# Weight pieces converted in blocks of two, and attention values split straight from PSUM, in an attention + mixture kernel

## The chip, the cores and the metric

The kernel runs on one core of a Trainium2 chip. The metric is the device time of one execution in microseconds (us). Before the change it is 828.13 us, the median of three runs (827.27 to 829.08). The core has a matrix engine (TensorE, PE in the profile; its weight loads are the row PEld), three engines for elementwise work (VectorE or DVE, ScalarE or ACT, GpSimd or POOL) and a queue that issues transfers between memory and the core (SyncE, SP). All of them run side by side, each in its own fixed order, and wait for each other through semaphores. Matmul results land in a memory of their own, PSUM; all other tiles lie in SBUF.

## The reference

There are 8 batches of 8 heads. Each head has 512 local and 32 global tokens of 64 numbers. A global token attends to all keys of its head; a local token attends to the 32 global keys and to the local keys at most 32 positions away. The result, laid out as 8 x 544 rows of 512, goes through three first-layer matrices whose maximum is taken, and one second-layer matrix:

```python
s_g = scale * np.matmul(q_g, k_all.transpose(0, 1, 3, 2))
out_g = np.matmul(sm(s_g), v_all)
mask = np.abs(pos[:, None] - pos[None, :]) <= window
s_l = np.concatenate([s_lg, np.where(mask, s_ll, -1000000000.0)], axis=-1)
out_l = np.matmul(sm(s_l), np.concatenate([v_g, v_l], axis=2))
...
h = np.maximum(np.maximum(x @ w1, x @ w2), x @ w3)   # 512 -> 768
return (h @ w_out).astype(np.float32)                # 768 -> 512
```

The four weight matrices arrive as 64-bit floating-point numbers (they are drawn as float32 and then multiplied with a float64 scale), and everything else as 32-bit.

## The kernel before, in words

**Split numbers.** Most products are made from operands of the type F32R (`fp32r` in the rows). The kernel splits an operand into a high part (a copy of that type) and a low part (the operand minus its high part), and a product is the sum of three matmuls: high x high, high x low, low x high. `copy` (line 105) makes the high part on ACT or DVE; `sub` (line 98) makes the low part on DVE or POOL, and on DVE alone if an operand lies in PSUM. Which engine is chosen is decided while the program is built: `least` (line 86) adds the cost of each choice to running loads of ACT ("a"), DVE ("d"), POOL ("p") and of a resource "x", counted by operations of DVE and POOL on SBUF, and takes the least. From the 26th tile on the first choice is always taken.

**Attention.** The work is cut into 128 tiles: a tile is one pair of heads and 128 of the 512 local queries. `SEQ` (line 209) is their order; in the first batch (16 tiles, `EARLY`) it is two tiles of each of the four head pairs, then the other two of each. The loop at line 567 does in iteration i, for tile SEQ[i]: transpose the probabilities of tile i+1 (`trans`, four PE transposes into one PSUM bank T, one copy to SBUF); score tile i+3 (`next_scores`, `scores`: matmuls into one of two PSUM banks S, then on DVE a masked row-minimum with L342, exponentials on ACT with L344, sums and reciprocals on DVE with L347 and L348, and a normalisation by `times`); multiply the probabilities of tile i with the values (`pv`, line 391: matmuls into O, a PSUM tile with one buffer, copied out into `xr`); load later queries, keys and values; run the weight steps; and split the attention output. From the second batch on the probabilities also make a way through a DMA (L351) before they are transposed.

**Matmuls of the mixture.** `moe_local(b)` is a generator that yields after each matmul; `fill(n)` takes n of them, 21 an iteration in the first 32 iterations (6, 5, 3 and 7). For batch 0 it starts in iteration 8 and does layer 1 for 256 columns, then for the other 256: 18 first-layer pieces, 12 matmuls each, over six tiles h0 to h5; then layer 2 with six second-layer pieces. It reads the attention output from `xs[0][p]`, one tile for each head pair, with a high and a low plane of 512 columns. In the first batch `split_x` makes it in every odd iteration, 256 columns of `xr` at a time: one `copy` and one `sub`.

**Weights.** Each of the 24 pieces is 128 x 512 float64 numbers (512 KB) and is turned into a split pair (`convert`, line 169): ACT takes the absolute value of the upper halves (L175); DVE clamps and shifts (L176, L177); one step later DVE merges the sign and the lower bits in (L180, L181); another step later a `copy` and a `sub` write the high and the low part over the raw piece. Scratch for the first 18 pieces is a pair of tiles that lie in h4 and h5, which layer 1 doesn't need yet, and for the last six the output buffers. `weight_step` (line 192) takes every piece in work one step on, begins the next and loads one more. `WS` (line 526) says how many weight steps an iteration makes: one in most, two in iterations 6, 10 and 14. Four pieces are loaded ahead of the loop, and a load of piece n waits for the ACT conversion of piece n-5.

**Order.** The program is written in the order above; while it is built a scheduler orders the instructions of each engine by that order and by when it estimates that their inputs are ready. So matmuls of the mixture can come ahead of attention work that isn't ready, and the lists on the engines follow the text only roughly.

## Time and profile before

| | |
|---|---|
| median of three runs | 828.13 us (827.27 to 829.08) |
| the profiled execution: its time, its span | 831.31 us, 829.5 us |
| busy time of PE | 803.7 us (97% of the span) |
| busy time of DVE, ACT, POOL | 616.8, 508.5, 459.2 us |
| share of the 16 DMA engines' time that the transfers of q1 took | 37.5% |
| DVE busy in the first 100 us, in fifths | 13.20, 19.65, 18.20, 19.54, 17.30 of 20 us each |
| PE busy in the same fifths | 14.13, 15.70, 17.60, 18.77, 17.87 |
| granted clock of PE in the same fifths | 1.00, 1.00, 0.83, 1.00, 0.91 |

Rows of a profile name a line of the kernel, an engine, the operation and its tiles, output first: `S<-kh,qn` is a score matmul that reads keys and queries. A bracket at the end of a timeline row is the idle time of the engine just before it and who ended it. `x18: 661/671/703` is a count, and least, median and longest duration in ns. DVE overlaps the end of one operation with the start of the next, so that a row's duration is somewhat longer than the distance to the next row's start (0.41 us against 0.33 where one at 23.70 us is followed by the next at 24.03). All times count from the start of the span.

### The profile page before, as it was taken

To read this page: it belongs to the slowest core of one execution; us is meant where nothing else is said; L and a number is where in the kernel's file an instruction comes from. 1 tells how busy PE (TensorE), PEld (TensorE's weight loads), DVE (VectorE), ACT (ScalarE), POOL (GpSimd) and SP (SyncE) were. 2 spreads that over 40 slices of the span, in tenths; PEclk is the share of its full clock that TensorE was granted. 3 is DMA by queue.
4 is the path that set the end of the run, shared out by engine and by line. 5 is a ranking of instruction groups with operands and counts; after the bars stand their busy time and mean duration, and the time that the engine had idled before them with its cause. 6 is when DMAs were issued, how large, how long until landed. Compare 5 with 4: busy or idle time off the path is not lost.

```text
span 829.5 us, 16594 instructions
## 1 busy us (share of the span) xinstructions
PE 803.7 (97%) x4772; PEld 685.8 (83%) x4772; DVE 616.8 (74%) x2192; ACT 508.5 (61%) x1415; POOL 459.2 (55%) x624
## 2 busy tenths in 40 slices
PE   7788999999999999999999999999999999999996
PEld 5577888888888888888888888888888888888895
DVE  6999897878888888888897888888887887421121
ACT  5987786657666766667676667666676766311110
POOL 4223345756677676756676676866786665311110
PEclk9989999999999999999999999999999999999999
DMA  9856554433334433343335333443325332100101
GB/s 309 304 185 212 167 152 148 139 127 115 109 115 136 121 92 112 99 151 102 104 109 166 116 98 92 133 138 110 93 88 166 115 93 74 61 1 1 38 14 26
DMA packets 97467, 98.16 MB, mean 118 GB/s; under 512 B 19296, under 2 KB 85856, under 8 KB 97376
## 3 DMA queue, kind: packets, MB, share of 16 engines
q1 hardware_dynamic: 97232, 96.87, 37.5%
q8 instruction: 38, 0.62, 0.3%
q14 instruction: 53, 0.43, 0.2%
q10 hardware_dynamic: 144, 0.23, 0.1%
HBM read 60.39 MB, written 8.91 MB: 84 GB/s over the span
## 4 chain that ended last, share of the span: by engine, by line
PE 86%; DMA 5%; issue 3%; DVE 2%; SPq 1%; ACT 1%; POOL 1%; POOLq 0%; DVEq 0%; ACTq 0%
PE pm L441 48%; PE pm L463 17%; PE O L409 7%; PE S L339 5%; PE T L362 2%; DMA prob<-s 2%; DMA raw<-w_in 2%; PE T L363 2%; PE S L289 2%; PE S L335 1%; DMA vraw<-v_in 1%; PE S L381 1%; PE O L401 1%; POOL w L103 1%; DMA qn<-q_in 1%
## 5 line engine op out<-in xcount | busy, mean ns | idle before, releaser
L441 PE MATMUL pm<-xs,w 128*128 128x512 f32 (+1 forms) x2160 | 488.9, 367 | 1.3 <-ACT m L115 0.9
L441 PEld LDWEIGHTS pm<-xs,w 128*128 128x128 f32 x2160 | 355.9, 191 | 52.7 <-issue 4.2
L463 PE MATMUL pm<-w,h 128*128 128x512 f32 x612 | 156.4, 396 | 0.0
L103 POOL TENSOR_TENSOR h<-m,h 128x512 fp32r<-128x512 f32 (+1 forms) x59 | 70.6, 1197 | 109.8 <-ACT h L115 109.2
L463 PEld LDWEIGHTS pm<-w,h 128*128 128x128 f32 x612 | 109.4, 188 | 19.1 <-issue 0.2
L450 DVE TENSOR_TENSOR m<-pm,m 128x512 f32<-128x512 f32 (+1 forms) x120 | 72.8, 607 | 63.1 <-PE pm L441 62.3
L344 ACT ACTIVATE s<-s,nm 128x192 f32<-128x192 f32 (+1 forms) x224 | 103.3, 462 | 22.3 <-DVE nm L342 17.6
L103 POOL TENSOR_TENSOR qs<-qraw,qs 128x256 fp32r<-128x256 f32 x100 | 76.5, 765 | 69.1 <-issue 33.2
L125 POOL TENSOR_SCALAR s<-s,z 128x224 f32<-128x224 f32 (+1 forms) x194 | 84.9, 446 | 36.5 <-ACT lox L115 18.9
L342 DVE CUSTOM_DVE_ANT_0 s<-S,mask 128x192 f32<-128x192 f32 (+1 forms) x224 | 74.8, 370 | 16.3 <-PE S L339 7.7
L103 POOL TENSOR_TENSOR vs<-vraw,vs 128x256 fp32r<-128x256 f32 x102 | 75.0, 736 | 13.3 <-ACT vs L115 6.5
L103 DVE TENSOR_TENSOR pt<-T,pt 128x512 fp32r<-128x512 f32 x102 | 70.4, 690 | 15.2 <-ACT pt L115 13.8
L409 PEld LDWEIGHTS O<-pt,vs 128*128 128x128 f32 x408 | 65.9, 188 | 10.4 <-issue 2.4
L409 PE MATMUL O<-pt,vs 128*128 128x320 f32 (+1 forms) x408 | 73.1, 300 | 1.4 <-DVE pt L103 1.4
L115 ACT CAST pt<-T 128x512 fp32r<-128x512 f32 x102 | 60.3, 592 | 16.6 <-PE T L363 14.0
L339 PEld LDWEIGHTS S<-kst,qs 128*128 128x128 f32 x400 | 59.6, 190 | 8.7
L417 DVE TENSOR_TENSOR xr<-O,lox 64x160 f32<-64x160 f32 x204 | 64.3, 315 | 2.9
L103 POOL TENSOR_TENSOR kst<-kraw,kst 64x576 fp32r<-64x576 f32 x44 | 63.9, 1453 | 4.3 <-PE S L335 1.0
L115 ACT CAST h<-m 128x512 fp32r<-128x512 f32 (+1 forms) x59 | 33.2, 562 | 52.8 <-DVE m L450 52.5
L115 ACT CAST qs<-qraw 128x256 fp32r<-128x256 f32 x93 | 38.0, 409 | 44.0 <-PE S L339 31.1
L339 PE MATMUL S<-kst,qs 128*128 128x192 f32 (+1 forms) x400 | 59.5, 270 | 0.0
L347 DVE TENSOR_SCALAR z<-z 128x1 f32<-128x1 f32 x256 | 37.2, 147 | 27.3 <-ACT s L344 18.7
(123 smaller groups left out, 1183.0 us busy)
## 6 DMA issues: line engine op xcount, KB each, us to landing
vraw<-v_in SPq DMA_DIRECT2D x122, 128.0 KB, 2.3
qraw<-q_in SPq DMA_DIRECT2D x100, 128.0 KB, 2.1
prob<-s SPq DMA_DIRECT2D x56, 224.0 KB, 2.5
raw<-w_in SPq DMA_DIRECT2D x24, 512.0 KB, 4.9
prob<-s SPq DMA_DIRECT2D x56, 192.0 KB, 2.3
out_dram<-o SPq DMA_DIRECT2D x32, 256.0 KB, 2.6
kraw<-k_in SPq DMA_DIRECT2D x25, 320.0 KB, 3.1
qn<-q_in SPq DMA_DIRECT2D x29, 128.0 KB, 3.7
```

Source lines behind the costliest of these rows:

```text
L103: (dve if least(c) == "d" else pool).tensor_tensor(out=out, in0=a, in1=b, op=ALU.subtract)
L115: act.copy(out=out, in_=a)
L125: pool.tensor_scalar(out=out, in0=a, scalar1=col, scalar2=1.0, op0=ALU.mult, op1=ALU.mult)
L339: pe.matmul(ph[j][:, 0:n], lhsT=qs[sl][:, a, 128 * j:128 * j + 128], rhs=kst[p][:, j, c0:c0 + n], start=(a == 0), stop=(a == 1))
L342: dve.tensor_tensor_reduce(out=s[:, j, 0:n], in0=ph[j][:, 0:n], in1=mask[:, (1, 0, 1, 0)[t], 32 * (t == 0):32 * (t == 0) + n], scale=-0.12 ...
L344: act.activation(out=s[:, j, 0:n], in_=s[:, j, 0:n], func=AF.Exp, bias=nm[:, j:j + 1], scale=-1.0, accum_out=z[:, j:j + 1])
L347: dve.tensor_scalar(out=z[:, j:j + 1], in0=z[:, j:j + 1], scalar1=1e-9, scalar2=None, op0=ALU.add)
L409: pe.matmul(o[:, j, 0:320].rearrange("p (a q) -> p a q", a=2)[:, :, 0:n], lhsT=vs[sl][:, 2 * j + c].rearrange("p a d -> p (a d)"), rhs=pt[ ...
L417: dve.tensor_tensor(out=xr[p][64 * j:64 * j + 64, t], in0=o[0:64, j, 0:160], in1=lo[:, j], op=ALU.add)
L441: pe.matmul(ps[:, 0:n], lhsT=weight(3 * f + i, w)[:, 128 * k:128 * k + 128], rhs=xs[k][:, a, c0:c0 + n], start=(q == 0), stop=(q == 11))
L450: dve.tensor_tensor(out=m[:, 0:n], in0=ps[:, 0:n], in1=m[:, 0:n], op=ALU.max)
L463: pe.matmul(banks[t], lhsT=hh[f][:, a, 128 * t:128 * t + 128], rhs=weight(18 + f, w), start=((f, a, w) == (0, 0, 0)), stop=((f, w) == (5, 1)))
```

## The change

**Weights.** The 18 first-layer pieces are loaded, converted and kept in nine blocks of two; the six second-layer pieces stay single. A block is one transfer of 1 MB, one ACT operation, four DVE operations, one `copy` and one `sub`, each over 1024 columns in place of two over 512. The scratch of block k is a fresh tile in h3, h4 or h5, by the list `PLACE`. A load of block k waits for the ACT conversion of block k-3, two blocks are loaded ahead of the loop in place of four pieces, and the next load goes out only in an iteration that begins a block. `weight_step` runs once in each iteration, and `WS` now lists the iterations that begin a block. What `convert` tells the planner it spends is changed to fit.

**First batch's values.** `pv` for the first 16 tiles no longer copies O into `xr`. It takes the tile's 128 columns of `xs[0][p]`: a `copy` out of PSUM writes the high plane, and a `sub` that reads O in PSUM and the high plane writes the low plane. The eight calls of `split_x` in the odd iterations go.

```diff
@@ -148,59 +148,66 @@
     raw, wt = {}, {}
 
     def weight(n, a):
-        return wt[n][:, 512 * a:512 * a + 512]
+        if n < 18:
+            return wt[n // 2][:, n % 2, 512 * a:512 * a + 512]
+        return wt[n - 9][:, 0, 512 * a:512 * a + 512]
 
     xg = const.tile([128, NP, B, SG], F32, name="xg")
     turned = psT.tile([128, 512], F32, name="T")
     dve.memset(turned, 0.0)
 
-    spare = [moe.tile([128, 2, 512], I32, name="spare", tag=f"h{f}") for f in (4, 5)]
+
+    PLACE = [3, 4, 5, 3, 4, 3, 5, 4, 5]
     loaded, marks = [0], {}
 
     def load_weight():
-        n = loaded[0]
-        if n < 24:
+        k = loaded[0]
+        if k < 15:
             loaded[0] += 1
-            raw[n] = const.tile([128, 512], mybir.dt.int64, name=f"raw{n}", tag=f"w{n}")
-            d = nc.sync.dma_start(out=raw[n], in_=win[n])
-            if n >= 6:
-                tc.add_manual_dep(d.ins, marks[n - 5], SYNC, reason="pace")
-
-    def convert(n):
-        r = raw[n].bitcast(I32).rearrange("p (n t) -> p n t", t=2)
-        if n < 18:
-            c = spare[n // 2 % 2 if n < 15 else 1][:, n % 2]
-        else:
-            c = moe.tile([128, 512], I32, name="wct", tag="o", bufs=2)
-        marks[n] = act.activation(out=f32(c), in_=f32(r)[:, :, 1], func=AF.Abs).ins.name
+            m = 2 if k < 9 else 1
+            raw[k] = const.tile([128, m, 512], mybir.dt.int64, name=f"raw{k}", tag=f"w{k}")
+            if m == 2:
+                d = nc.sync.dma_start(out=raw[k], in_=win[2 * k:2 * k + 2].rearrange("t p x -> p t x"))
+            else:
+                d = nc.sync.dma_start(out=raw[k][:, 0], in_=win[k + 9])
+            if k >= 3:
+                tc.add_manual_dep(d.ins, marks[k - 3], SYNC, reason="pace")
+
+    def convert(k):
+        r = raw[k].bitcast(I32).rearrange("p j (n t) -> p j n t", t=2)
+        if k < 9:
+            c = moe.tile([128, 2, 512], I32, name="wct", tag=f"h{PLACE[k]}")
+        else:
+            c = moe.tile([128, 1, 512], I32, name="wct", tag="o", bufs=2)
+        m = 2 if k < 9 else 1
+        marks[k] = act.activation(out=f32(c), in_=f32(r)[:, :, :, 1], func=AF.Abs).ins.name
         dve.tensor_scalar(out=f32(c), in0=f32(c), scalar1=2.0 ** -15, scalar2=HIMAX, op0=ALU.max, op1=ALU.min)
         dve.tensor_scalar(out=c, in0=c, scalar1=0x07FFFFFF, scalar2=3, op0=ALU.bitwise_and, op1=ALU.logical_shift_left)
-        spend("a", 520)
+        spend("a", 427 * m + 98)
         yield
-        dve.scalar_tensor_tensor(out=c, in0=r[:, :, 1], scalar=-0x40000000, in1=c, op0=ALU.bitwise_and, op1=ALU.bitwise_or)
-        dve.scalar_tensor_tensor(out=c, in0=r[:, :, 0], scalar=29, in1=c, op0=ALU.logical_shift_right, op1=ALU.bitwise_or)
-        spend("dx", 1900)
+        dve.scalar_tensor_tensor(out=c, in0=r[:, :, :, 1], scalar=-0x40000000, in1=c, op0=ALU.bitwise_and, op1=ALU.bitwise_or)
+        dve.scalar_tensor_tensor(out=c, in0=r[:, :, :, 0], scalar=29, in1=c, op0=ALU.logical_shift_right, op1=ALU.bitwise_or)
+        spend("dx", 1600 * m + 300)
         yield
-        wt[n] = const.tile([128, 1024], F32R, name=f"w{n}", tag=f"w{n}")
-        copy(weight(n, 0), f32(c))
-        sub(weight(n, 1), f32(c), f32(weight(n, 0)))
+        t = wt[k] = const.tile([128, m, 1024], F32R, name=f"w{k}", tag=f"w{k}")
+        copy(t[:, :, 0:512], f32(c))
+        sub(t[:, :, 512:1024], f32(c), f32(t)[:, :, 0:512])
         yield
 
-    todo = iter(range(24))
+    todo = iter(range(15))
     live = []
 
-    def weight_step():
+    def weight_step(begin):
         for c in list(live):
             next(c[0])
             c[1] += 1
             if c[1] == 3:
                 live.remove(c)
-        n = next(todo, None)
-        if n is not None:
-            c = convert(n)
+        if begin:
+            c = convert(next(todo))
             next(c)
             live.append([c, 1])
-        load_weight()
+            load_weight()
 
 
     NS = 4 * B * NP
@@ -392,15 +399,21 @@
         p, t = divmod(sl, 4)
         pt = pts.pop(sl)
         o = psO.tile([128, 2, 512], F32, name="O")
-        if t == 0:
+        if t == 0 and sl < EARLY:
+            xs.setdefault(0, []).append(x_tile())
+        elif t == 0:
             xr[p] = xp.tile([128, 4, 160], F32, name="xr")
         if sl < NAT:
 
             for c, j in ((0, 0), (0, 1), (1, 0), (1, 1)):
                 n = 160 if sl >= EARLY and c < GCH[t][2] else 128
                 pe.matmul(o[64 * j:64 * j + 64, 0, 0:n], lhsT=vraw[sl][:, 2 * j + c], rhs=pt[:, j, c, 0:n], start=(c == 0), stop=(c == 1))
-            n = 160 if sl >= EARLY else 128
-            copy(xr[p][:, t, 0:n], o[:, 0, 0:n], True)
+            if sl < EARLY:
+                x = xs[0][p]
+                copy(x[:, 0, 128 * t:128 * t + 128], o[:, 0, 0:128], True)
+                sub(x[:, 1, 128 * t:128 * t + 128], o[:, 0, 0:128], f32(x)[:, 0, 128 * t:128 * t + 128], True)
+            else:
+                copy(xr[p][:, t], o[:, 0, 0:160], True)
         else:
 
             for j in range(2):
@@ -523,7 +536,7 @@
 
     mm = [None]
 
-    WS = [1, 1, 1, 1, 1, 1, 2, 1, 1, 1, 2, 1, 1, 1, 2, 1, 1, 1, 1, 1, 1, 1, 1, 1]
+    WS = [0, 2, 4, 6, 7, 9, 10, 12, 14, 15, 16, 17, 18, 19, 20]
 
     def fill(n):
         if mm[0]:
@@ -556,13 +569,11 @@
     load_v(SEQ[1], 1)
     load_weight()
     load_half(2)
-    load_weight()
     next_scores(1)
     load_v(SEQ[2], 2)
     load_weight()
     next_scores(2)
     load_v(SEQ[3], 3)
-    load_weight()
     trans(SEQ[0])
     for i, sl in enumerate(SEQ):
         p, t = divmod(sl, 4)
@@ -608,13 +619,8 @@
             load_v(tile_at(i + 4), i + 4)
         else:
             load_v(tile_at(i + 4))
-        for _ in range(WS[i] if i < len(WS) else 0):
-            weight_step()
+        weight_step(i in WS)
         if i < 16:
-            if i % 2:
-                if i < 8:
-                    xs.setdefault(0, []).append(x_tile())
-                split_x(xr[p][:, 2 * (i // 8):2 * (i // 8) + 2, 0:128], xs[0][p], 256 * (i // 8), 256)
             if i == 7:
                 mm[0] = moe_local(0)
         elif i % 16 >= 12:
```

## The prediction

> **What bounds the kernel now.** The page comes first: TensorE (PE) is busy 97% of the span, so the whole run is worth at most the 25.8 us in which it isn't, and work taken from another engine counts only where PE waits for it.
>
> ```profile
> span 829.5 us, 16594 instructions
> PE 803.7 (97%) x4772; PEld 685.8 (83%) x4772; DVE 616.8 (74%) x2192; ACT 508.5 (61%) x1415; POOL 459.2 (55%) x624
> ```
>
> The view by stretches says where that is. Columns: stretch, its length, busy us of PE, PEld, VectorE (DVE), ScalarE (ACT), GpSimd (POOL), granted clock, DMA share, GB/s.
>
> ```profile
> 0.00:17.00 17.00, 11.13 (x67) 9.21 (x68) 10.25 (x54) 9.26 (x29) 6.01 (x22) 1.00 0.89 300
> 17.00:38.60 21.60, 18.04 (x125) 12.54 (x123) 21.20 (x73) 18.95 (x53) 6.23 (x7) 1.00 0.94 323
> 38.60:43.50 4.90, 1.75 (x13) 1.17 (x14) 4.90 (x15) 3.92 (x11) 1.62 (x1) 0.88 0.36 129
> 43.50:50.60 7.10, 7.10 (x35) 6.55 (x35) 7.10 (x27) 6.21 (x18) 2.25 (x2) 0.61 0.25 76
> 50.60:75.00 24.40, 24.00 (x184) 20.52 (x184) 22.60 (x79) 20.33 (x59) 6.07 (x7) 1.00 0.78 258
> 75.00:100.00 25.00, 22.05 (x160) 18.15 (x159) 21.84 (x74) 17.57 (x54) 8.36 (x8) 0.93 0.57 180
> 165.00:820.00 655.00, 654.48 (x3672) 561.13 (x3671) 473.94 (x1663) 386.25 (x1062) 390.43 (x534) 1.00 0.32 98
> ```
>
> From 165 us on PE has no gap; nothing this change touches lies there. From 17 to 50.6 us DVE is the full engine (33.2 of 33.6 us). After PE's idle stretch at 38.6 the granted clock is 0.61 over 7.1 us, 2.8 us of PE work lost; 75 to 100 loses 1.8 (0.07 of 25).
>
> The timeline of PE shows what it waits for.
>
> ```profile
> 35.57 0.65 PE L401 MATMUL O<-pt,vn 128*64 128x128 f32 x6
> 38.62 0.66 PE L401 MATMUL O<-pt,vn 128*64 128x128 f32 x8 [0.84 <-ACT xr L115]
> 40.63 1.02 PE L335 MATMUL S<-kh,qn 128*128 128x224 f32 x4 [1.36 <-DVE nm L342]
> 43.43 0.47 PE L362 MATMUL T<-one,early 128*128 128x128 f32 x1 [1.77 <-ACT early L123]
> 60.83 0.44 PE L401 MATMUL O<-pt,vn 128*64 128x128 f32 x4 [0.38 <-ACT xr L115]
> 80.08 0.62 PE L441 MATMUL pm<-xs,w 128*128 128x256 f32 x3 [0.91 <-ACT m L115]
> 82.37 0.28 PE L362 MATMUL T<-identr,prob 128*128 128x128 f32 x1 [1.67 <-DMA prob<-s]
> 95.05 0.26 PE L362 MATMUL T<-identr,prob 128*128 128x128 f32 x1 [0.35 <-DMA prob<-s]
> ```
>
> And the timeline of DVE says why: the first row-minimum (L342) of tiles 9, 10, 11, 13, 14, 15 and 17, counted in the order of work.
>
> ```profile
> 33.67 0.34 DVE L342 CUSTOM_DVE_ANT_0 early<-S,mask 128x192 f32<-128x192 f32 x1
> 39.87 0.38 DVE L342 CUSTOM_DVE_ANT_0 early<-S,mask 128x224 f32<-128x224 f32 x1
> 43.96 0.34 DVE L342 CUSTOM_DVE_ANT_0 early<-S,mask 128x192 f32<-128x192 f32 x1
> 52.12 0.35 DVE L342 CUSTOM_DVE_ANT_0 early<-S,mask 128x192 f32<-128x192 f32 x1
> 59.63 0.38 DVE L342 CUSTOM_DVE_ANT_0 early<-S,mask 128x224 f32<-128x224 f32 x1
> 64.43 0.34 DVE L342 CUSTOM_DVE_ANT_0 early<-S,mask 128x192 f32<-128x192 f32 x1
> 73.13 0.39 DVE L342 CUSTOM_DVE_ANT_0 s<-S,mask 128x224 f32<-128x224 f32 x1
> ```
>
> Tile 11 comes 4.1 us after tile 10, an ordinary distance; but tile 10 comes 6.2 us after tile 9, and tile 14 7.5 us after tile 13. Between those two pairs lie the iterations i=6 and i=10, where WS asks for two weight steps. Tile i+3 is scored in iteration i, ahead of that iteration's value product and weight step, so the minimum of tile i+4 stands behind weight step i. Both waits of PE at 40 to 43 us hang on tile 10; the one at 82.37 hangs on tile 17.
>
> **Blocks of two on DVE.** The time from one DVE start to the next gives the cost of an operation in a full queue.
>
> ```profile
> 20.02 0.15 DVE L348 RECIPROCAL z<-z 128x1 f32<-128x1 f32 x1
> 20.09 0.13 DVE L347 TENSOR_SCALAR z<-z 128x1 f32<-128x1 f32 x1
> 23.70 0.41 DVE L176 TENSOR_SCALAR spare<-spare 128x512 f32<-128x512 f32 x1
> 24.03 0.15 DVE L348 RECIPROCAL z<-z 128x1 f32<-128x1 f32 x1
> 27.88 0.68 DVE L103 TENSOR_TENSOR w<-spare,w 128x512 fp32r<-128x512 f32 x1
> 28.48 0.15 DVE L348 RECIPROCAL z<-z 128x1 f32<-128x1 f32 x1
> ```
>
> A one-column operation costs 0.07, so that is the fixed part; a clamp or shift (L176, L177) 0.33; a subtraction, or either merge (L180, L181, whose shortest forms last the same 0.67), 0.60. A piece takes 2 x 0.33 + 2 x 0.60 + 0.60 = 2.46. On twice the columns a clamp costs 2 x 0.33 - 0.07 = 0.59, a merge or subtraction 1.13, a block 4.57 against 4.92 for two pieces: 0.35 saved, 3.15 over nine blocks.
> The Trainium skill, "VectorE: DVE Perf Modes", gives (N+151)/0.96 ns for a 32-bit tensor_tensor, a fixed part of 0.157 us; by it the nine blocks would save 45 x 0.157 = 7.1 us, an estimate, the wait at 82.37 would go whole (1.67 instead of 1.5) and the sum below would be -2.5 instead of -2.3. The 0.07 between the starts above speaks against that page's figure for operations in a full queue.
>
> The order matters more. Summed over all steps up to i (clamps begun, merges one step later, subtraction one after that), old against new: i=6: 17.3, 14.9 (-2.4, ahead of tile 10); i=7: 19.7, 18.3 (-1.4, tile 11); i=9: 24.7, 24.0 (-0.6, tile 13); i=10: 29.6, 27.5 (-2.1, tile 14); i=11: 32.0, 30.9 (-1.2, tile 15); i=13: 37.0, 35.4 (-1.5, tile 17); i=14: 41.9, 37.7 (-4.1); i=15: 44.3, 40.7 (-3.7, tile 19). The doubled steps go, but steps 7 and 8 become heavier (3.4 each instead of 2.5), so the lead comes and goes.
>
> **Values split from PSUM.** Eight copies and eight subtractions of 256 columns go; seven and the copies have rows up to 80 us:
>
> ```profile
> L115 ACT CAST xs<-xr x8: 401/404/410, 14.9 to 79.9; 128x256 fp32r<-128x256 f32 x8
> L103 DVE TENSOR_TENSOR xs<-xr,xs x4: 409/410/413, 25.1 to 51.4; 128x256 fp32r<-128x256 f32 x4
> L103 POOL TENSOR_TENSOR xs<-xr,xs x3: 931/1030/1058, 15.4 to 67.3; 128x256 fp32r<-128x256 f32 x3
> L113 DVE COPY xr<-O x2: 281/282/282, 12.8 to 26.1; 128x128 f32<-128x128 f32 x2
> ```
>
> Sixteen subtractions of 128 columns out of PSUM come, all on DVE. No row has one; the copy out of the same bank lasts 0.28, the subtraction of 256 columns 0.41, so one lies between 0.28 and 0.41, less 0.08 of overlap: 0.20 to 0.33, taken at 0.20 as its columns equal the copy's. Fourteen up to tile 17 cost 2.8 (4.6 at the other end), four at 0.33 go (1.3), and so does what three POOL operations did to DVE:
>
> ```profile
> 18.28 1.27 POOL L103 TENSOR_TENSOR w<-spare,w 128x512 fp32r<-128x512 f32 x1 [0.41 <-DVE w L113]
> 18.33 1.77 DVE L180 SCALAR_TENSOR_TENSOR spare<-raw,spare 128x512 int32<-128x512 int32 x1
> ```
>
> Here a merge that lasts 0.67 alone ends 0.55 after POOL does: it stood still for 1.1. At about 0.5 for each shorter xs operation that is 1.5, so this part is +0.0 on DVE (0 to +1.8). ACT loses 8 x 0.40 = 3.2 us. Its cover is gone only at 80.08, where PE waits 0.91 for a copy on ACT; I take half, -0.45 (0 to -0.91).
>
> **Loads, buffers, other queues.** The first block must land whole. The first row is from the chain of waits (start, length), the last from the list of waits (us in total, times, longest).
>
> ```profile
> 5.48 6.40 DMA raw<-w_in
> 9.26 0.67 ACT L175 ACTIVATE spare<-raw 128x512 f32<-128x512 f32 x1 [0.25 <-DMA raw<-w_in]
> SPq L250 <- DMA raw<-w_in: 4.0, 5, 1.4
> ```
>
> Piece 1 landed at 11.88, so ACT's first conversion starts up to 2.6 later, and the exponentials of tiles 2 and 3 queue behind it on ACT if they are placed so. DVE is idle 6.75 us before 17 us and covers it: 0, at worst +2.6. Query loads on SP waited 4.0 us for weight landings; a block of 1 MB takes 0.5 MB at 300 GB/s = 1.7 us longer, while nine issues go; 0, at worst +1.7. Two issues ahead of the loop go; the queries, keys and values behind each block load stand behind one piece more than they did, and none at the iterations without a load. A block load waits for the conversion of the block three before it, which has long run when it is issued, so SP loses nothing to that wait. The single pieces of the second layer are loaded one or two iterations later than before, four of them in iterations 15 to 18 in place of two, beside the reshuffle of the probabilities through the DMA queue; the DMA share is 0.57 there, and I take 0. The converter also borrows h3, but its block is done at i=11, and layer 1, which gets 6+5+3+7 = 21 matmuls in each iteration from i=8, first writes h3 after 144 of them, near i=8+144/21 = 14.9: no wait.
>
> **Sum.** The wait at 82.37 is 1.67 long and its chain comes 1.5 earlier: -1.5. The wait at 95.05, 3.7 earlier: -0.35. ACT: -0.45. The gain at 40 us (up to 2.1 and a share of the clock) I count at nothing: DVE's lead is 0.6 again by tile 13, and PE can't run further ahead than the later tiles let it. Together -2.3 from the profiled 831.31 is 829.0. That execution stood 3.18 above the median of the runs, 828.13; on their scale the forecast is **825.8**.
>
> **Rivals.**
> *Stalls vanish, much faster.* Tile 10 is 2.1 earlier, so 3.13 us of waits shrink to 1.0, the clock doesn't drop (2.8) and later waits go as in the sum: 2.1 + 2.8 + 2.3 = 7.2 below the median, 821; where the clock drops all the same, 4.4, 823.7. For: the waits lie where the doubled step ended. Against: the leads at tiles 11 to 13. 13%.
>
> *Longer GpSimd subtractions, no change.* The planner keeps sending weight subtractions to POOL; 1.27 for 512 columns becomes about 2.5, and a DVE operation behind it stands still for up to 1.9 instead of 2 x 0.74. Four such blocks before tile 17 cost 1.6: the lead of 1.5 is gone. What remains is -0.35: 827.8. Merges are the first to suffer, and the minima queue behind them. For: the pair of rows at 18.3. Against: by the planner's own formulas a subtraction of 1024 columns counts 2455 on POOL and 1140 on DVE, so DVE must be ahead by twice as much as before until POOL is chosen. 19%. The Trainium skill, "SBUF — State Buffer", summary of rules for kernel authors, says that the second of the two engines to issue "fully blocks" until the first ends; the rows at 18.3 agree.
>
> *PE tied to DVE through O, slower.* O has one buffer. Now it is free once ACT copied; after, once DVE also subtracted, and DVE's subtraction for product i stands behind the minimum of tile i+3. Product 13 starts at 60.83, but the subtraction for product 12 would come after tile 15's minima, 64.43 + 0.6; with 1.2 of lead product 13 starts at 64.1: 3.3 late. Product 9 (38.62) would wait for tile 11 (43.96), but there PE idles anyway. The matmuls, transposes and scores queued behind product 13 are late with it; 2.58 of waits at 80 and 82 absorb part, and with -1.5 no longer to be had 0.7 to 3.3 remains, say +2.0: 830.1. It decides where DVE is more than one iteration behind PE. For: the two rows. Against: the order of PE is drawn up anew, and first-layer matmuls can go ahead of product 13. 26%.
>
> **How the numbers follow.** Forecast 42% (its own range 824.3 to 827.3), the rivals 13, 19 and 26%. 0.2% (1.66 us) is about what a measurement can tell from no change: below 826.47 is faster, above 829.79 slower. Faster: 0.31 of the forecast, 0.13, 0.01 = 0.45. Same: 0.11, 0.14 of the second, 0.03 of the third = 0.28. Slower: 0.04 and 0.23 = 0.27. The range, 822.5 to 831.0, leaves out the lower half of the first rival (6 or 7%) and the dear end of the third with a late start on top (another 10%).
>
> **What would show it.** Right: the minima of tiles 10, 14 and 17 come 2, 2 and 1.5 us earlier, steps between minima are even, merges of 1024 columns last 1.2, and the wait before tile 17's transposes is under 0.3. Wrong: value products that wait for a DVE subtraction of xs after 50 us; merges of 3 us beside POOL; a first conversion that holds exponentials at 10 us; or a 100 us mark (the time at which PE's gapless run begins) that didn't move.

## The result

The changed kernel takes 837.57 us (median, 836.56 to 839.26), beside 828.61 us (827.27 to 830.83) for the kernel before on the same chip. The ratio is 1.0112, with a 95% interval of 1.0097 to 1.0128: some 9 us slower, where 2.3 us faster was forecast. Three executions of the experiments below, two of e8 and one of the kernel before, took 972 to 2657 us and are in no ratio here.

The profiled execution took 838.2 us, 6.9 more than that of before (831.31). As that one stood about 3 us above its median, the two profiles show about 7 of the 9 us. The page's span and busy row after:

```profile
span 836.4 us, 16503 instructions
PE 803.8 (96%) x4772; PEld 686.5 (82%) x4772; DVE 614.5 (73%) x2166; ACT 505.9 (60%) x1388; POOL 465.6 (56%) x614
```

TensorE is busy for the same 803.7 to 803.8 us with the same 4772 matmuls. So the longer span is idle time of PE: 32.6 us in place of 25.8. DVE is busy for 2.3 us less and ACT for 2.6 less, as the change meant, POOL for 6.4 more, and nothing saved reached the end. The view by stretches, with the columns and stretches of the prediction's:

```profile
0.00:17.00 17.00, 10.33 (x58) 8.12 (x59) 9.97 (x50) 7.72 (x23) 4.77 (x20) 1.00 0.87 287
17.00:38.60 21.60, 16.91 (x118) 12.64 (x117) 18.32 (x66) 16.17 (x42) 10.00 (x7) 0.92 0.88 307
38.60:43.50 4.90, 3.11 (x13) 2.30 (x13) 4.90 (x12) 3.63 (x10) 1.66 (x1) 0.80 0.63 248
43.50:50.60 7.10, 5.79 (x44) 4.48 (x42) 5.15 (x12) 4.12 (x9) 2.37 (x1) 0.90 0.04 7
50.60:75.00 24.40, 21.34 (x147) 18.47 (x147) 21.94 (x60) 18.17 (x48) 7.48 (x4) 0.86 0.64 219
75.00:100.00 25.00, 20.99 (x163) 17.88 (x162) 24.18 (x80) 19.21 (x55) 9.31 (x6) 1.00 0.64 203
165.00:820.00 655.00, 653.15 (x3662) 559.21 (x3661) 474.89 (x1689) 390.32 (x1072) 396.36 (x538) 1.00 0.33 99
```

In the first 100 us PE idles 21.5 us, against 15.9 before (the lengths less the PE column, summed). That is 5.6 of the 6.8; another 1.3 lies between 165 and 820 us. The granted clock falls in other places than before: it is 0.86 from 50.6 to 75 us (3.4 us of work) and was 0.61 from 43.5 to 50.6 (2.8). The telling column is DVE's: from 17 to 50.6 us it was full before (33.2 of 33.6), and now it works 28.37 of 33.6. PE idles more while the engine that bounded it idles too: now the engines wait for one another in turn. The list of waits from 8 to 100 us says for whom DVE waits, first after, then before (us in total, times, longest):

```profile
DVE z L354 <- ACT early L351: 6.4, 10, 1.7
```

```profile
DVE z L347 <- ACT early L344: 0.8, 2, 0.4
```

Ten times DVE stands at the sums of a tile whose exponentials ACT hasn't done; before it was five times, with three waits of 2.2 us in total for the exponentials of tiles named `s`. The timeline of PE after, its longer waits from 20 to 90 us and the one of tile 17's transposes, at 88.07:

```profile
24.47 1.44 PE L454 MATMUL pm<-xs,w 128*128 128x256 f32 x5 [1.82 <-POOL w L103]
32.49 0.74 PE L454 MATMUL pm<-xs,w 128*128 128x256 f32 x4 [0.97 <-POOL w L103]
...
41.22 0.82 PE L342 MATMUL S<-kh,qn 128*128 128x224 f32 x2 [1.50 <-DVE nm L349]
51.25 0.33 PE L369 MATMUL T<-one,early 128*128 128x128 f32 x1 [1.91 <-ACT early L123]
...
68.64 0.33 PE L369 MATMUL T<-one,early 128*128 128x128 f32 x1 [2.03 <-ACT early L123]
85.92 1.69 PE L454 MATMUL pm<-xs,w 128*128 128x256 f32 x12 [0.89 <-DVE m L113]
88.07 0.25 PE L369 MATMUL T<-identr,prob 128*128 128x128 f32 x1 [0.46 <-DMA prob<-s]
89.94 0.28 PE L388 MATMUL S<-identr,probg 128*128 128x128 f32 x1 [1.39 <-DMA probg<-sg]
```

They hang on five different things: the low part of a weight block on POOL, the minima of a tile on DVE, normalised probabilities on ACT, a copy on DVE and transfers. None of these waits is for DVE's subtraction of `xs`, which the third rival was about.

How a tile comes late shows in the timelines of tile 8, DVE first and then POOL:

```profile
29.89 0.38 DVE L349 CUSTOM_DVE_ANT_0 early<-S,mask 128x224 f32<-128x224 f32 x1
...
30.57 2.42 DVE L185 TENSOR_SCALAR wct<-wct 128x1024 int32<-128x1024 int32 x1
...
33.03 0.38 DVE L349 CUSTOM_DVE_ANT_0 early<-S,mask 128x224 f32<-128x224 f32 x1
```

```profile
30.08 2.36 POOL L103 TENSOR_TENSOR w<-wct,w 128x1024 fp32r<-128x1024 f32 x1 [2.83 <-ACT w L115]
```

The shift of a weight block stands between the two row-minima of one tile, and beside POOL's 2.36 us it lasts 2.42 instead of 0.68. The second minimum comes 3.14 us after the first, and what follows it in that tile (exponentials, normalisation, transposes) can only come later still. The same with tile 10, shown further down, ends in the wait of 1.50 at 41.22. The groups of the scratch tile `wct`, the value products' `xs` and the first conversion (ns: least, median, longest):

```profile
L184 DVE TENSOR_SCALAR wct<-wct x15: 405/682/2549, 13.5 to 114.3; 128x1024 f32<-128x1024 f32 x9, 128x512 f32<-128x512 f32 x6
L188 DVE SCALAR_TENSOR_TENSOR wct<-raw,wct x15: 673/1216/2492, 16.0 to 118.3; 128x1024 int32<-128x1024 int32 x9, 128x512 int32<-128x512 int32 x6
...
L103 POOL TENSOR_TENSOR w<-wct,w x12: 1278/2362/2656, 22.1 to 115.8; 128x1024 fp32r<-128x1024 f32 x8, 128x512 fp32r<-128x512 f32 x4
```

```profile
L103 DVE TENSOR_TENSOR xs<-O,xs x16: 269/282/291, 13.3 to 85.8; 128x128 fp32r<-128x128 f32 x16
```

```profile
12.28 1.14 ACT L183 ACTIVATE wct<-raw 128x1024 f32<-128x1024 f32 x1
```

An unhindered clamp takes 0.68 us and a merge 1.21, a subtraction out of PSUM 0.28: the prediction's prices. But POOL got eight of the nine block subtractions, and the first conversion starts at 12.28 instead of 9.26.

### The profile page after: what moved, and what is told of

The parts are those of the page before. It is cut to its first block, busy times and chain, and to the rows that moved or that the text cites. A ratio compares the mean times of both kernels' runs of the same rounds, so it can differ in the third digit from the quotient of the medians.

```text
span 836.4 us, 16503 instructions
## 1 busy us (share of the span) xinstructions
PE 803.8 (96%) x4772; PEld 686.5 (82%) x4772; DVE 614.5 (73%) x2166; ACT 505.9 (60%) x1388; POOL 465.6 (56%) x614
## 4 chain that ended last, share of the span: by engine, by line
PE 83%; DVE 7%; ACT 3%; DMA 2%; issue 2%; POOL 2%; SPq 1%; ACTq 0%; DVEq 0%; POOLq 0%
PE pm L454 46%; PE pm L476 16%; PE O L422 6%; PE S L346 5%; PE T L369 2%; DMA prob<-s 2%; PE T L370 2%; PE S L342 1%; PE S L296 1%; DVE wct L188 1%; DVE wct L185 1%; DVE wct L189 1%; POOL w L103 1%; PE S L388 1%; DVE s L349 1%
## 5 line engine op out<-in xcount | busy, mean ns | idle before, releaser
L125 POOL TENSOR_SCALAR s<-s,z 128x224 f32<-128x224 f32 (+1 forms) x186 | 82.1, 450 | 35.6 <-ACT lox L115 17.8
L115 ACT CAST h<-m 128x512 fp32r<-128x512 f32 (+1 forms) x59 | 33.2, 562 | 52.8 <-DVE m L463 52.4
L115 ACT CAST qs<-qraw 128x256 fp32r<-128x256 f32 x87 | 35.5, 409 | 41.2 <-PE S L346 28.8
```

What stands on the lines that cost most here:

```text
L115: act.copy(out=out, in_=a)
L125: pool.tensor_scalar(out=out, in0=a, scalar1=col, scalar2=1.0, op0=ALU.mult, op1=ALU.mult)
```

## The experiments

Eighteen runs, told as differences from the kernel before or from one another. The last column is (ratio - 1) x 828.13, so that all stand on one scale, whichever runs of the kernel before they were compared with.

| run | what it is | ratio to before, 95% interval | us above before |
|---|---|---|---|
| | the change | 1.0112 [1.0097, 1.0128] | 9.3 |
| e1 | blocks, without the values part | 1.0098 [1.0079, 1.0117] | 8.1 |
| e2 | values part alone | 1.0054 [1.0034, 1.0075] | 4.5 |
| e3 | the change, block subtraction on DVE | 1.0097 [1.0080, 1.0114] | 8.0 |
| e4 | the change, operations halved | 1.0182 [1.0148, 1.0216] | 15.1 |
| e5 | before, pieces begun in pairs | 1.0025 [1.0007, 1.0044] | 2.1 |
| e6 | e1, high part a step earlier | 1.0120 [1.0081, 1.0160] | 9.9 |
| e7 | before, one charge of the planner changed | 1.0056 [1.0038, 1.0075] | 4.6 |
| e8 | e2 with two halves of O | 1.0031 [1.0012, 1.0050] | 2.6 |
| e9 | e5 with loads of 1 MB | 1.0038 [1.0025, 1.0052] | 3.1 |
| e10 | e1 with loads of 512 KB | 1.0124 [1.0101, 1.0147] | 10.3 |
| e11 | before, another charge changed | 1.0084 [1.0066, 1.0101] | 7.0 |
| e12 | e1 with kept scratch | 1.0082 [1.0061, 1.0103] | 6.8 |
| e13 | e9 with fresh scratch | 1.0048 [1.0027, 1.0068] | 4.0 |
| e14 | e9 with the values part | 1.0153 [1.0133, 1.0173] | 12.7 |
| e15 | the change with kept scratch | 1.0084 [1.0063, 1.0106] | 7.0 |
| e16 | e9, one charge changed | 1.0116 [1.0079, 1.0153] | 9.6 |
| e17 | e1, one charge changed | 1.0096 [1.0074, 1.0117] | 8.0 |
| e18 | e9, another charge changed | 1.0098 [1.0073, 1.0122] | 8.1 |

The expectations number the theories in the order in which they came up; here each is called by what it says.

**The parts alone (e1, e2).** e1 takes `pv` and the calls of `split_x` back to the kernel before:

```diff
-            if sl < EARLY:
-                x = xs[0][p]
-                copy(x[:, 0, ...], o[:, 0, 0:128], True)
-                sub(x[:, 1, ...], o[:, 0, 0:128], f32(x)[:, 0, ...], True)
-            else:
-                copy(xr[p][:, t], o[:, 0, 0:160], True)
+            n = 160 if sl >= EARLY else 128
+            copy(xr[p][:, t, 0:n], o[:, 0, 0:n], True)
```

> Blocks of two as in the change; the first batch's values go through xr and split_x as before. The change measured 9.0 us over the kernel before (837.57 against 828.61). Theory 1 (the loss is the 2.36 us subtractions on GpSimd, which got 8 of 9 blocks: they hold back two-input and fast operations of DVE and the first-layer matmuls): 834 to 838, nearly all of the loss. Theory 2 (the loss is in the values: O is held until DVE has subtracted, and DVE waits in its queue for ACT's copy): near the kernel before, 826 to 830. Theory 3 (long operations of any engine and the late first block): also 834 to 838.

e2 makes the opposite edit in the kernel before:

```diff
-            n = 160 if sl >= EARLY else 128
-            copy(xr[p][:, t, 0:n], o[:, 0, 0:n], True)
+            if sl < EARLY:
+                x = xs[0][p]
+                copy(x[:, 0, ...], o[:, 0, 0:128], True)
+                sub(x[:, 1, ...], o[:, 0, 0:128], f32(x)[:, 0, ...], True)
+            else:
+                copy(xr[p][:, t], o[:, 0, 0:160], True)
...
-                split_x(xr[p][...], xs[0][p], 256 * (i // 8), 256)
```

> The kernel before, with only the value products of the first batch split straight from PSUM. Theory 1 and 3: 826 to 830, as this part leaves the weight operations alone. Theory 2: 833 to 838, with PE waiting for O or DVE waiting for ACT's copy in the first 80 us.

Measured 8.1 and 4.5 us above before: each part loses by itself, and 12.6 together is more than the change's 9.3. The timeline of e1 from 48 to 57 us, all engines, shows two of its stalls:

```profile
48.38 1.15 ACT L183 ACTIVATE wct<-raw 128x1024 f32<-128x1024 f32 x1 [1.35 <-DVE w L103]
49.43 0.79 ACT L123 ACTIVATE early<-early,z 128x192 f32<-128x192 f32 x2
...
49.93 0.33 PE L369 MATMUL T<-one,early 128*128 128x128 f32 x1 [1.75 <-ACT early L123]
...
52.30 2.56 POOL L103 TENSOR_TENSOR w<-wct,w 128x1024 fp32r<-128x1024 f32 x1 [7.28 <-ACT w L115]
...
52.54 2.60 DVE L103 TENSOR_TENSOR xs<-xr,xs 128x256 fp32r<-128x256 f32 x1
...
56.44 0.88 ACT L123 ACTIVATE early<-early,z 128x224 f32<-128x224 f32 x2 [2.51 <-DVE z L354]
...
56.98 0.47 PE L369 MATMUL T<-one,early 128*128 128x128 f32 x1 [2.76 <-ACT early L123]
```

First a conversion of 1.15 us stands on ACT ahead of a normalisation that PE waits for. Then a subtraction on DVE that lasts 0.41 alone lasts 2.60 beside POOL's block; the sums of a tile stand behind it, with a shift of 1.14 us between them, and PE idles 2.76 us. The Trainium skill, "SBUF — State Buffer", summary of rules for kernel authors, says that where VectorE's operation has two inputs in SBUF and GpSimd's reads SBUF, the second to issue "fully blocks" until the first finishes; this pair of rows agrees, 2.60 beside 2.56.

**GpSimd's long subtraction (e3).** In the change, the low part of a block always goes to DVE:

```diff
-        sub(t[:, :, 512:1024], f32(c), f32(t)[:, :, 0:512])
+        if m == 2:
+            spend("dx", 1140)
+            dve.tensor_tensor(out=t[:, :, 512:1024], in0=f32(c), in1=f32(t)[:, :, 0:512], op=ALU.subtract)
+        else:
+            sub(t[:, :, 512:1024], f32(c), f32(t)[:, :, 0:512])
```

> The whole change, but the low part of each block of two is always subtracted on DVE (1.2 us each) and never on GpSimd. Theory 1: most of the loss comes back, 827 to 831; the stretched 1024-column operations (mean 1.1 us for a clamp of 0.68) become 0.68 and 1.2, and first-layer matmuls no longer wait for a weight. Theory 2: no better than the change, 836 to 839. Theory 3: DVE holds even more long operations, 836 to 840.

Measured 8.0, against 9.3 for the change; the intervals overlap. So the 2.4 us on POOL, visible as they are in single stalls, are at most a small part of what the change costs: without them other stalls add up to nearly the same.

**Half operations (e4).** The blocks, their loads and steps stay, but each operation of a block is made as two of 512 columns:

```diff
-        marks[k] = act.activation(out=f32(c), in_=f32(r)[:, :, :, 1], func=AF.Abs).ins.name
-        dve.tensor_scalar(out=f32(c), in0=f32(c), scalar1=2.0 ** -15, ...)
-        ...
+        for j in range(m):
+            h = c[:, j]
+            marks[k] = act.activation(out=f32(h), in_=f32(r)[:, j, :, 1], func=AF.Abs).ins.name
+            dve.tensor_scalar(out=f32(h), in0=f32(h), scalar1=2.0 ** -15, ...)
+            ...
```

> The whole change (blocks of two in loading, scratch and schedule of the steps, values from PSUM), but each conversion operation is issued as two of 512 columns instead of one of 1024. Theory 1 and 3: 827 to 831, since each subtraction on GpSimd is 1.27 us again and every operation short. Theory 2: 835 to 839. If the late landing of the first block of 1 MB is the cause, also 835 to 839, and the first clamp starts near 13.5 us as in the change.

Measured 15.1, the slowest of all. Short operations, in the change's steps and with its values part, bring nothing back.

**The rhythm alone (e5), and the copy earlier (e6).** e5 keeps the operations of the kernel before and the size of its loads, and begins pieces two at a time, in the change's iterations and scratch tiles:

```diff
-    WS = [1, 1, 1, 1, 1, 1, 2, 1, 1, 1, 2, 1, 1, 1, 2, 1, ...]
+    WS = [2, 0, 2, 0, 2, 0, 2, 2, 0, 2, 2, 0, 2, 0, 2, 1, 1, 1, 1, 1, 1]
...
-            c = spare[n // 2 % 2 if n < 15 else 1][:, n % 2]
+            c = spare[PLACE[n // 2]][:, n % 2]
```

> The kernel before (single pieces, loads of 512 KB, operations of 512 columns, values through xr), with only the rhythm of the change: pieces 2k and 2k+1 begin in the same iteration, the iterations of the change's list, one weight step per iteration, scratch in h3, h4 and h5. Theory 4 (the loss comes from the rhythm: the conversions and copies of a pair, 2.2 to 2.6 us on ACT, all fall into the iterations that begin one, ahead of the exponentials, and none into the others): 836 to 841, since the run with half operations lay at 843.4 and the values alone cost 4.3. Theory 1 and 3 (long operations, GpSimd, landing of 1 MB): 826 to 831.

e6 is e1 with the high part of a block copied in the step of the merges, which spreads ACT's work:

```diff
-        yield
         t = wt[k] = const.tile([128, m, 1024], F32R, ...)
         copy(t[:, :, 0:512], f32(c))
+        yield
```

> Blocks alone (836.5), with the high-part copy of a block issued one step earlier, right behind its merges, so that ACT has a conversion in one iteration and a copy in the next instead of both in one. Theory 4: 829 to 833. If the length of the operations or GpSimd's 2.4 us is what counts: 835 to 838. If the copy now waits on ACT for the merges with the exponentials behind it: above 837.

e5 measured 2.1: the rhythm costs a little at most. e6 measured 9.9, no better than e1's 8.1.

**Edits that change no operation (e7, e11).** The planner is told other costs, in the kernel before; all its operations, loads and steps stay.

```diff
-        spend("a", 520)
+        spend("a", 620)
```

> The kernel before with one number of the planner changed (a conversion is charged 620 instead of 520 on ACT): the operations, steps and loads stay the same, some copies and subtractions change engine and the orders on DVE and ACT shift. If the kernel before is no better than its neighbours: within 827 to 830. If its order is a favourable one among many (theory 5): 830 to 835, and then an edit's few us can't be put down to its operations alone.

```diff
-        spend("dx", 1900)
+        spend("dx", 1700)
```

> A second kernel that differs from the one before in one number of the planner (the merges are charged 1700 instead of 1900 on DVE), with the same operations. Theory 5 (the order of the kernel before is a favourable one): 830 to 836 again. If the first such run hit a bad order by chance: 827 to 830.

Measured 4.6 and 7.0 us above before: a half and three quarters of what the change costs, for edits that remove and add nothing. What they alter is on which engine `least` puts a few operations, and with it the order of the rest. By its page e7 has 2194 instructions on DVE where before has 2192, and 1413 on ACT for 1415. e7's first 100 us are much those of before, with the same stalls 0.4 us later (39.02, 41.05 and 43.84 for 38.62, 40.63 and 43.43); the waits that cost it come after. The timeline of PE in e7:

```profile
103.63 0.59 PE L513 MATMUL S<-one,side 64*128 64x64 f32 x6 [0.95 <-POOL side L125]
113.95 0.92 PE L335 MATMUL S<-kn,qn 128*128 128x192 f32 x4 [1.05 <-ACT pt L115]
136.58 0.69 PE L339 MATMUL S<-kst,qs 128*128 128x192 f32 x4 [1.04 <-DVE nmg L293]
```

The first 100 us and the stretch after them in the view by stretches, e7 first, then before:

```profile
0.00:100.00 100.00, 85.09 (x577) 68.78 (x578) 85.86 (x317) 74.80 (x214) 30.44 (x44) 0.95 0.72 240
100.00:165.00 65.00, 60.14 (x505) 51.95 (x504) 54.52 (x209) 43.46 (x133) 36.97 (x46) 1.00 0.46 136
```

```profile
0.00:100.00 100.00, 84.07 (x578) 68.15 (x579) 87.89 (x317) 76.25 (x219) 30.54 (x45) 0.95 0.72 240
100.00:165.00 65.00, 62.29 (x514) 54.51 (x513) 54.27 (x213) 45.42 (x136) 38.25 (x46) 0.97 0.47 143
```

From 100 to 165 us PE works 2.15 us less in e7, at a clock of 1.00 in place of 0.97, and begins nine matmuls fewer; the two spans are 3.5 us apart (833.0 and 829.5). So this loss doesn't lie where the change's does: in the first 100 us PE idles 14.9 us in e7, 16.5 in e11 and 15.9 before, but 21.5 after the change.

**O held longer (e8).** e2, with the two halves of the PSUM tile O used in turn in the first batch:

```diff
-        o = psO.tile([128, 2, 512], F32, name="O")
+        if sl < EARLY:
+            if not halves:
+                halves.append(psO.tile([128, 2, 512], F32, name="O"))
+            o = halves[0][:, SEQ.index(sl) % 2:SEQ.index(sl) % 2 + 1]
+        else:
+            o = psO.tile([128, 2, 512], F32, name="O")
```

> Values alone (832.8), with O's two halves used in turn by the first batch's products, so that a product doesn't wait for the subtraction of the one before. Theory 2 (O held until DVE has subtracted costs the 4.3 us): 828 to 830. If the extra operations on DVE or their order cost it: 831 to 834.

Measured 2.6 against e2's 4.5, with overlapping intervals. A cost of O being held can't be told from none.

**Loads and scratch (e9, e10, e12, e13, e15).** e9 is e5 with the change's loads of 1 MB, e10 is e1 with loads of single pieces, four ahead:

```diff
-            d = nc.sync.dma_start(out=raw[n], in_=win[n])
+            if m == 2:
+                d = nc.sync.dma_start(out=raw[k], in_=win[2 * k:2 * k + 2].rearrange("t p x -> p t x"))
```

> The pairs of pieces (831.4, every operation of 512 columns) with the loads of the change: transfers of 1 MB, two ahead of the loop, a load after each pair that begins, paced by the conversion three blocks before. Theory 6 (the block loads cost most: pieces come later, and on SP's queue the queries and values stand behind them): 836 to 841. If the length of the operations costs it: 830 to 833.

```diff
-            if m == 2:
-                d = nc.sync.dma_start(out=raw[k], in_=win[2 * k:2 * k + 2].rearrange("t p x -> p t x"))
+            k, j = (n // 2, n % 2) if n < 18 else (n - 9, 0)
+            ...
+            d = nc.sync.dma_start(out=raw[k][:, j], in_=win[n])
```

> Blocks alone (836.5, operations of 1024 columns) with every piece loaded by a transfer of its own, 512 KB, four pieces ahead of the loop and each paced by the conversion of the piece five before, as in the kernel before. Theory 6: 828 to 832. If the length of the operations costs it: 835 to 838.

Large loads cost the pairs 1.0 us (3.1 against 2.1, overlapping), and small loads help the blocks by nothing (10.3 against 8.1). The first conversion is the clearest miss of the prediction in the trace. In e9 it starts at 12.27, as late as in the change, and e9 is only 3.1 above before, so its lateness isn't the price either. (e10 says nothing on that point: its first conversion takes a whole block and starts at 12.54.)

e12 (from e1) and e15 (from the change) keep three scratch tiles in place of a fresh one per block; e13 gives e9 a fresh one per pair:

```diff
+    spare = {f: moe.tile([128, 2, 512], I32, name="spare", tag=f"h{f}") for f in (3, 4, 5)}
...
-            c = moe.tile([128, 2, 512], I32, name="wct", tag=f"h{PLACE[k]}")
+            c = spare[PLACE[k]]
```

> Blocks alone (836.5; operations of 1024 columns, 1 MB loads) with the scratch in three tiles kept throughout, as the pairs have it, instead of a fresh tile for each block. If the length of the operations is the cause: 834 to 839. Theory 7 (the fresh scratch is the cause): 829 to 833.

> The whole change with the kept scratch. Theory 7: 830 to 834. If the length of the operations is the cause, as the change: 836 to 840.

```diff
-            c = spare[PLACE[n // 2]][:, n % 2]
+            if j == 0:
+                spare[k] = moe.tile([128, 2, 512], I32, name="wct", tag=f"h{PLACE[k]}")
+            c = spare[k][:, j]
```

> Pairs of pieces with 1 MB loads (831.6; operations of 512 columns) with a fresh scratch tile for each pair in h3, h4 or h5. If the length of the operations is the cause: 829 to 834. Theory 7: 835 to 841.

Kept scratch: 6.8 against 8.1, and 7.0 against 9.3; fresh scratch in pairs: 4.0 against 3.1. Each time the fresh tiles are 0.9 to 2.3 us slower, and each time the intervals overlap.

**Values on pairs (e14).** e9 with the values part, the same edit as e2's:

```diff
-            copy(xr[p][:, t, 0:n], o[:, 0, 0:n], True)
+                copy(x[:, 0, ...], o[:, 0, 0:128], True)
+                sub(x[:, 1, ...], o[:, 0, 0:128], f32(x)[:, 0, ...], True)
```

> Pairs of pieces with 1 MB loads and kept scratch (831.6) plus the values split straight from PSUM: everything the run with half operations had but the fresh scratch (843.4). If the two parts add up (the values alone cost 4.3): 834 to 838. If the fresh scratch cost the rest there: also 834 to 838. If the rhythm and the values hurt each other: 840 to 846.

Measured 12.7. The same edit costs 9.6 on pairs (e14 less e9), 4.5 on the kernel before, and 1.2 or 0.2 on blocks (the change less e1, e15 less e12). A cost of its own operations, whatever the order, would be about the same each time.

**The order disturbed in pairs and in blocks (e16, e17, e18).** By then pairs of pieces without the values part lay at 2.1 to 4.0 and all kernels with blocks in long operations at 6.8 to 10.3, which looked like a price of long operations. The charge changes of e7 and e11 are made in e9, and one in e1:

```diff
-        spend("a", 520)
+        spend("a", 620)
```

> The kernel with pairs of pieces and 1 MB block loads (e9, measured at 1.0038 of the kernel before, 831.6 us), in which the planner is told 620 instead of 520 ns of ScalarE for each piece; the operations are the same, their order is not (278 lines of difference in the order of TensorE's work). If merging two operations into one long one costs about 5 us whatever the order, pairs stay clear of blocks in a disturbed order too: 829 to 834 us, below every block kernel so far (836.1 to 839.2). If the gap between pairs and blocks is one more draw among orders, as the two runs with a changed planner number on the kernel before suggest (+4.7 and +6.8 us), this lands anywhere from 830 to 840, and a time of 836 or more would mean that the gap isn't a price of long operations.

```diff
-        spend("a", 427 * m + 98)
+        spend("a", 427 * m + 198)
```

> The blocks without the values part (e1, measured at 1.0098, 836.5 us), in which the planner is told 100 ns more of ScalarE for each block or piece; same operations, 172 lines of difference in TensorE's order. If long operations set the price, 835 to 840 us again. If the order does, anything from 829 to 841 us; a time below 834 would mean that blocks can come as cheap as pairs.

```diff
-        spend("dx", 1900)
+        spend("dx", 1700)
```

> The same pairs of pieces (e9, 831.6 us) with the planner's charge for a piece's merges on VectorE lowered from 1900 to 1700 ns; same operations, 294 lines of difference in TensorE's order. Long operations as the price: 829 to 834 us, below the blocks. The order as the price: anything from 830 to 840 us; 836 or more would speak against a fixed price of long operations.

Measured 9.6 and 8.1 for the pairs, 8.0 for the blocks. In the totals the gap is gone: pairs of short operations in another order are as slow as blocks. And here the loss does lie in the first batch. The first 100 us, e9 and then e16:

```profile
0.00:100.00 100.00, 84.15 (x580) 67.44 (x581) 89.56 (x322) 75.96 (x216) 33.23 (x47) 0.97 0.73 240
```

```profile
0.00:100.00 100.00, 78.82 (x541) 61.30 (x542) 87.25 (x306) 71.24 (x200) 34.93 (x46) 0.98 0.69 231
```

PE idles 15.9 us there in e9, 21.2 in e16 and 19.1 in e18. In the waits of PE up to 100 us, e9 and then e16:

```profile
PE T L369 <- ACT early L123: 1.2, 3, 0.5
```

```profile
PE T L369 <- ACT early L123: 3.8, 4, 2.5
```

The longest of them in e16, on the timeline of all engines:

```profile
37.76 0.35 DVE L349 CUSTOM_DVE_ANT_0 early<-S,mask 128x192 f32<-128x192 f32 x1
...
38.04 1.82 DVE L182 TENSOR_SCALAR spare<-spare 128x512 f32<-128x512 f32 x2
38.04 1.53 POOL L103 TENSOR_TENSOR w<-spare,w 128x512 fp32r<-128x512 f32 x1 [1.94 <-ACT w L115]
...
39.78 0.68 DVE L103 TENSOR_TENSOR w<-spare,w 128x512 fp32r<-128x512 f32 x1
40.38 0.20 DVE L354 TENSOR_SCALAR z<-z 128x1 f32<-128x1 f32 x2
...
41.09 0.80 ACT L123 ACTIVATE early<-early,z 128x192 f32<-128x192 f32 x2 [0.67 <-DVE z L355]
...
41.59 0.33 PE L369 MATMUL T<-one,early 128*128 128x128 f32 x1 [2.51 <-ACT early L123]
```

Three weight operations of 512 columns stand between a tile's minima and its sums. The two clamps take 1.82 us where each lasts 0.41 alone, as one of them stands beside POOL, and PE idles 2.51 us. It is the stall of e1 at 56.98, made of short operations.

## Why the prediction was wrong

**The bound** was read rightly: PE's idle time in the first batch is most of what moved (5.6 of 6.8 us in the first 100). The long run from 165 us on, where the prediction saw nothing that the change touches, lost 1.3.

**The prices of single operations** held. Clamp 0.68 and merge 1.21 on 1024 columns; 0.28 for a subtraction out of PSUM, the copy's own duration, as taken. The totals on the page, 2.3 us less for DVE and 2.6 for ACT, are no test of these prices: DVE is busy for 611.5 us in e7 and 620.3 in e11, against 616.8 before, with the same operations.

**The step that failed is "The order matters more".** It counted how much weight work lies ahead of each tile in the text of the program, took the difference as a lead of DVE (2.4 at tile 10, 1.5 at tile 17), and carried that lead to PE's waits at 82.37 and 95.05: 1.85 of the 2.3. That supposes that DVE's work ahead of a tile sets the tile's time, and that the rest of every queue stays as it is and moves up. The lead itself came, and was larger. What DVE spends on the weights' scratch tile ahead of tile 17's first minimum, `spare` before and then `wct` after (stretch, its length, busy us of DVE, clock, DMA share, GB/s):

```profile
0.00:73.13 73.13, 45.79 (x72) 0.95 0.77 259
```

```profile
0.00:79.05 79.05, 39.90 (x33) 0.91 0.71 242
```

DVE had at least 5.9 us less of this work to do, partly because POOL took eight of nine block subtractions while the prediction's count has them all on DVE. Yet the tile's minimum came 5.9 us later (79.05 for 73.13), where 1.5 earlier was forecast. Two things ate the lead. Other work came to DVE, fourteen subtractions and six copies out of PSUM among it, so that DVE's whole work ahead of the tile was the same (64.23 us, 64.18 before); the prediction had put the values at +0.0. And DVE idled 5.9 us more than before on the way, almost all of it for ACT's exponentials (6.4 us up to there, against 0.8). The timeline of DVE after, the minima of tile 10 and the first of tile 14:

```profile
38.07 0.38 DVE L349 CUSTOM_DVE_ANT_0 early<-S,mask 128x224 f32<-128x224 f32 x1
...
38.51 2.29 DVE L185 TENSOR_SCALAR wct<-wct 128x1024 int32<-128x1024 int32 x1
...
40.80 0.36 DVE L349 CUSTOM_DVE_ANT_0 early<-S,mask 128x224 f32<-128x224 f32 x1
...
62.61 0.38 DVE L349 CUSTOM_DVE_ANT_0 early<-S,mask 128x224 f32<-128x224 f32 x1
```

Tile 10's first minimum, which "What would show it" wanted 2 us earlier, did come 1.8 earlier (39.87 before), but its second stands behind a shift of 2.29 us, and tile 14's first is 3 us later, not 2 earlier (59.63 before). The wait before tile 17's transposes did shrink, to 0.46 at 88.07 from 1.67 at 82.37; it comes 5.7 us later. So this sign came about in another way than forecast: the tile wasn't earlier, but PE was ready for it 6.9 us later (87.61 for 80.70). The 0.45 for ACT fails with it: the wait of 0.91 at 80.08 for a copy of `m` on ACT came back as one of 0.89 for a copy of `m` on DVE, at 85.92.

**What took its place** is in part the order as such; that it is all of it isn't shown. The kernel before has a favourable order: seven kernels (e5, e7, e9, e11, e13, e16, e18) do its operations on its sizes in another order, five of them also with other steps, scratch or loads; all seven are slower, and two charges alone cost it 4.6 and 7.0 us. The pairs lost 6.5 and 5.0 to the same charges (e16 and e18 less e9). The blocks lost nothing to their one charge (8.0 against 8.1), which fits an order that was bad already, and a price of the blocks as well. So a new draw of the order costs about 5 to 7 us where the order was good, against a saving of 2.3 that the operations were said to bring. The change's 9.3 lies 2.3 to 4.7 above the two draws of the kernel before, and the blocks spread over 3.5 us among themselves (6.8 to 10.3).

Where the loss lies speaks for the order less clearly than the totals do. In the first 100 us of the one profile of each kernel, PE idles 14.9 to 16.6 us in all that keep the weight steps of the kernel before (before, e2, e7, e8, e11), whatever their order. It idles 15.9 to 21.2 in the pairs without the values part and 18.8 to 26.6 in the eight kernels with long blocks. The disturbed pairs (e16, e18) lose there, by the order alone, as much as some of the blocks. But no kernel with long blocks came under 18.8, so a price of long operations in that stretch isn't ruled out.

**The second rival** ("Longer GpSimd subtractions") was argued away by the planner's own charges, 2455 against 1140, which should have made POOL's share smaller; it took eight of nine blocks, as against nine of 18 pieces. The stretching came as described, 2.42 and 2.60 us. The weight given to it did not: e3 takes those operations off POOL and ends at 8.0 against 9.3, with overlapping intervals.

**The third rival** named the side (slower), but not for its reason as far as the trace shows: no matmul of the changed kernel's first 100 us waits over 0.6 us for O or for DVE's `xs` (DVE itself waited 1.51 once for ACT's copy, before 29.08), and e8, whose products alternate between two halves of O, can't be told from e2.

**"Loads, buffers, other queues"** was taken at zero. The first conversion came 3.0 us later, a little more than its worst case of 2.6, and e9 shows no price for it that can be measured.

**The range** left out what came: the third rival mentions that PE's order is drawn up anew, but no rival made that a loss of several microseconds that belongs to no single operation.

**Open.** How much of the loss is long operations, held buffers or values in a given order can't be said, as the order can't be held while the operations change; writing the order of all five queues by hand was not tried. Nor is it known what makes the order of the kernel before good, beyond the waits that it lacks. The values part on pairs (e14 12.7, and e4 15.1, which has both too) lies 2.4 us or more above every other kernel; whether that is more than a bad draw is open. No kernel tried is faster than the one before.

## What to carry to other kernels

Before an edit of some microseconds is believed or blamed in a program whose queues a planner orders, change a number of the planner that alters no operation, two or three times: that spread, here 4.6 to 7.0 us, is the least that an edit must beat. See also in which stretch it falls: in the kernel before it fell after the first 100 us, while the change's loss lay within them. A lead counted on one engine's work reaches the end only if the other queues keep their order; where they are drawn up anew, sum nothing, and widen the range by that spread on the side where the present order is better than its neighbours. And when one kernel of a group looks cheap, disturb its order as well before its difference from the others is called a price: here a price of 5 us for long operations, borne out by ten kernels, could no longer be told from the order after two edits of one number each in the cheap one.

## What was not expected of the hardware

A 256-column subtraction on DVE that lasts 0.41 us alone lasted 2.60 beside a POOL operation of 2.56 (e1 at 52.54), and a shift of 0.68 lasted 2.42 beside 2.36 (the change at 30.57): the DVE operation stood until the POOL operation that had begun before it was done. With 1024 columns on POOL a single DVE operation lost 2.19 and 1.74 us; the merge in the prediction, beside 512 columns on POOL, lost 1.1. Halving the operations didn't shorten the program (15.1 against 9.3 us), and moving them to DVE didn't clearly (8.0).
